# Fourteen products of ones on TensorE in the first stage of a fused attention and feed-forward kernel

## The chip, the core and the metric

The kernel runs on one core of a Trainium2 chip. The metric is the device time of one execution in microseconds; below, "us" means that. A run's time is the median of several executions; the profile shows one more execution, with its own time.

## What is computed

The inputs are q, k and v of 4 batches, 8 heads, 1152 positions and 64 dimensions, and two weight matrices. Neighbouring rows of q are averaged, so 576 rows of scores stand for each head:

```python
q_pool = q.reshape(B, H, S // 2, 2, D).mean(axis=3)
scores = np.matmul(q_pool, k.transpose(0, 1, 3, 2)) / np.sqrt(D)
attn = softmax(scores)                       # rows, max subtracted
x = np.matmul(attn, v).transpose(0, 2, 1, 3).reshape(B * S // 2, H * D)
h = x @ w_in                                 # 2304x512 by 512x2048
out = np.maximum(h, 0.0) ** 2 @ w_out        # 2304x512
```

## The kernel before

The work falls into 16 pairs of heads (4 batches by 4 pairs), each cut into nine chunks of 128 rows of scores, 144 chunks in all. A chunk goes through a fixed series of steps: a score product S on TensorE, a row bound MX on VectorE, the exponential EX on ScalarE, a transpose of the result P, and, for a group of chunks, the product with v. Behind the attention, and mixed into it, nine blocks of 256 rows go through the feed-forward part (lines 1032 and 1081 hold its products).

Pair 0 is treated in full 32-bit precision from the start. The load LK of k comes in three pieces (line 384), that of q (LQ) in one (line 376). KX (line 422) transposes k on TensorE in three groups of six products with the identity, and KC (lines 414 and 416) copies each to SBUF. QS (line 399) adds neighbouring rows of q on VectorE, QY (line 435) transposes the sums in two groups, and QC copies them. Then the first score group S (line 652) makes two chunks at once, and VectorE's bound MX (line 684) and ScalarE's exponential EX (line 708) follow. For the pairs 0 to 3, P is transposed on TensorE in three groups of three, TP (line 749), and copied by TC (line 759 on ScalarE, 761 on VectorE).

The pairs 1 to 4 also have bound products GR (line 465): nine products of the raw k (or q, or v) with itself, whose largest entry, read by GM (line 469) on VectorE, gives a scale. GR of k for pair 1 is the first of them; it waits for that pair's load of k (line 369). That load uses the buffer of pair 0's k, and so waits for the last KX.

Beside this the weights are loaded (line 1135) and turned from 64-bit to 32-bit numbers, in steps W0, W1, W2, W4, W5 for w_in and U0 to U5 for w_out, on ScalarE (lines 1143, 1149, 1162), VectorE (line 1152, the combine at line 1168, line 1177) and GpSimd.

All these steps are listed with what they depend on, and the string `ORDER` gives the one sequence in which they are put out, with the engine of each and the buffer or PSUM bank that it takes. So every engine has a fixed order of its own and waits only for data and buffers. TensorE's first steps are KX 0, KX 1, KX 2, QY 0, QY 1, S of the chunks 0 and 1, GR of k for pair 1, TP 0 and TP 1 of chunk 0, S of the chunks 2 and 3, TP 0 of chunk 1. On SyncE's queue the loads of pair 0's k and q and of the first piece of w_in stand first; then come k of pair 1, a piece of w_in, one of w_out, and q of pair 1. Two PSUM banks, called a, serve KX, QY, GR, TP and most else; a step takes one through `bank(o)`, and the step that has read it gives it back. `ones` is a column of 128 ones of 16-bit type, written by VectorE at line 1325, and `cfg(k, d)` reads an entry of the table CFG.

Of the kernel before, what the change touches and what calls it, by code (L numbers as in the profile page):

```python
# [16 lines left out]
AX = mybir.AxisListType  # L17
PSUM = bass.MemoryType.PSUM

CFG = {'SPLIT': 0, 'TURN': [], 'TURNB': [], 'WDP': ((1, 0), (1, 1), (1, 2), (1, 3)), 'WSP': 0.4394, 'WOF': 23.2581, 'MSP': 10.7319, 'FV': (0, 1, 2, 3), 'PART': 1, 'QXD': (1, 2, 3, 4), 'MSC': (0, 1, 2, 3, 4, 5, 6, 7, 8, 9, 10, 11, 12, 13, 14, 15), 'FS': (0,), 'NSG': (12, 13, 14, 15)}  # L20


def cfg(k, d):
    return CFG.get(k, d)

# [117 lines left out]
def kernel(  # L143
# [12 lines left out]
    nc = tc.nc  # L156
# [27 lines left out]
    ones = c_p.tile([128, 1], BF16, name="ones")  # L184
# [56 lines left out]
    def bank(o, *shape):  # L241
        r, x = plan.slot[o["name"]]
        t = banks[r][x]
        if not shape:
            return t
        return t[:, : shape[0] * shape[1]].rearrange("p (a b) -> p a b", a=shape[0])

    def buf(*key):
        r, x = plan.slot[key]
        return bufs[r][x]  # L250

    def raw(*key):
        return raws[plan.slot[key][1]]
# [41 lines left out]
    def qT(n):  # L295
        s = preps[n]["slot"]
        return qTs[s] if s is not None else buf("qT", n).rearrange("p (l c m) -> p l c m", l=2, c=9)

    def k4(n):
        return kT(n).rearrange("p a b -> p (a b)").bitcast(F32).rearrange("p (c k) -> p c k", c=9)  # L300

    def q4(t):
        return t.rearrange("p l c m -> p (l c m)").bitcast(F32).rearrange("p (c m) -> p c m", m=64)
# [43 lines left out]
    def prep(n):  # L347
# [11 lines left out]
        def rk():  # L359
            return raw("k", n).rearrange("p (h c d) -> p h c d", h=2, c=9)  # L360
# [47 lines left out]
        if n in full_s:  # L408
            assert not keep
            kt4, qt4 = k4(n), q4(qT(n))  # L410

            def move(o, out, x):
                if o["eng"] == "ACT":
                    nc.scalar.activation(out, x, AF.Copy)
                else:
                    nc.vector.tensor_copy(out, x)

            def kx(o, x):
                tl["kx", n, x] = t = bank(o, 3, 128)
                for y in range(3):  # L420
                    for h in range(2):
                        nc.tensor.matmul(
                            t[h * 64 : h * 64 + 64, y], lhsT=rk()[:, h, 3 * x + y, :], rhs=ident,
                            start=True, stop=True, skip_group_check=True,
                        )

            def kc(o, x):
                move(o, kt4[:, 3 * x : 3 * x + 3], tl.pop(("kx", n, x)))

            def qy(o, z):  # L430
                tl["qy", n, z] = t = bank(o, 5, 64)
                for y in range(5 - z):
                    for h in range(2):
                        hs = slice(h * 64, h * 64 + 64)
                        nc.tensor.matmul(t[hs, y], lhsT=rq()[:, 5 * z + y, 0, :], rhs=ident[:, h : h + 127 : 2], start=True, stop=True, skip_group_check=True)

            def qc(o, z):
                t = tl.pop(("qy", n, z))
                if z == 0:
                    move(o, qt4[:, :5], t)  # L440
                else:
                    move(o, qt4[:, 5:8], t[:, :3])
                    for h in range(2):
                        hs = slice(h * 64, h * 64 + 64)
                        move(o, qt4[hs, 9 + h], t[hs, 3])

            add(("QS", n), qse, [("LQ", n)], qsum, need)
            for x in range(3):
                add(("KX", n, x), {"PE": 1270}, [("LK", n) + ((x,) if n == 0 and x < 2 else ())] + old, lambda o, x=x: kx(o, x), need, take=(("KX", n, x), ("a",), 0), give=("k", n) if x == 2 else None)
                add(("KC", n, x), alt("KC", ACT=380, DVE=460), [("KX", n, x)] + old, lambda o, x=x: kc(o, x), need, give=("KX", n, x))  # L450
            for z in range(2):
                add(("QY", n, z), {"PE": 760 - 150 * z}, [("QS", n)] + old, lambda o, z=z: qy(o, z), need, take=(("QY", n, z), ("a",), 0), give=("q", n) if z else None)
                add(("QC", n, z), alt("QC", ACT=350 + 350 * z, DVE=400 + 300 * z), [("QY", n, z)] + old, lambda o, z=z: qc(o, z), need, give=("QY", n, z))
        gram_ = cfg("GR0", 1) <= n < cfg("GRN", 5)

        if gram_:

            def gram(o, i, nm):
                if ("acc", n) not in tl:
                    tl["acc", n] = sm_p.tile([128, 3], F32, tag="acc", name="acc", bufs=2)  # L460
                p = bank(o, 1, 128)
                t = raw(nm, n).bitcast(BF16).rearrange("p (f t) -> p f t", t=2)[:, :, 1]
                for c in range(9):
                    x = t[:, c * 128 : (c + 1) * 128]
                    nc.tensor.matmul(p[:, 0], lhsT=x, rhs=x, start=(c == 0), stop=(c == 8))
                tl["gm", n, nm] = p

            def gmax(o, i, nm):
                nc.vector.reduce_max(tl["acc", n][:, i : i + 1], tl.pop(("gm", n, nm)), axis=AX.X)

            for i, nm in enumerate("kqv"):
                if nm not in todo:
                    continue
                L = "L" + nm.upper()
                add(("GR", n, nm), {"PE": 560}, [(L, n)], lambda o, i=i, nm=nm: gram(o, i, nm), need, take=(("GR", n, nm), ("a",), 0))
                add(("GM", n, nm), {"DVE": 200}, [("GR", n, nm)], lambda o, i=i, nm=nm: gmax(o, i, nm), need, give=("GR", n, nm))
            if "q" in todo:
                add(("QS", n), qse, [("GR", n, "q")], qsum, need)
            fdep = [("GM", n, nm) for nm in "kqv"]
        else:  # L480

            def sq(o, i, nm):
                if ("acc", n) not in tl:
                    tl["acc", n] = sm_p.tile([128, 3], F32, tag="acc", name="acc", bufs=2)
                src = rq()[:, :, 0, :] if nm == "q" else rk() if nm == "k" else rv()
                if nm == "v":
                    j = v2s[slot][:, :, :, 0, :].bitcast(BF16)
                else:
                    j = buf(nm + "2", n)[:, :1152].bitcast(BF16).rearrange("p (h c d) -> p h c d", h=2, c=9)
                    j = j[:, 0] if nm == "q" else j  # L490
                nc.scalar.activation(j, src, AF.Square, accum_out=tl["acc", n][:, i : i + 1])

            if "k" in todo:
                add(("QS", n), qse, [("LQ", n)], qsum, need)
                add(("QK", n), {"ACT": 1200}, [("LK", n)], lambda o: sq(o, 0, "k"), need, take=ktake)
            if "v" in todo:
                add(("QV", n), {"ACT": 1200}, [("LV", n)] + oldv, lambda o: sq(o, 2, "v"), need)
            if "q" in todo:
                add(("QQ", n), {"ACT": 700}, [("QS", n)], lambda o: sq(o, 1, "q"), need, take=qtake)
            fdep = [("QK", n), ("QQ", n), ("QV", n)]  # L500
# [123 lines left out]
    def chunk(i):  # L624
# [117 lines left out]
        if n in full_v:  # L742
            pt = pslot(vi, j, True)

            def tp4(o, x):
                t = bank(o, 3, 128)
                for y in range(3):
                    c = 3 * x + y
                    nc.tensor.matmul(  # L749
                        t[:, y], lhsT=P()[:, c * 128 : (c + 1) * 128], rhs=ident, is_transpose=True,  # L750
                        start=(y == 0), stop=(y == 2), skip_group_check=True,
                    )
                tl["tp", i, x] = t

            def tc4(o, x):
                t = tl.pop(("tp", i, x))
                out = pt[:, 3 * x : 3 * x + 3]
                if o["eng"] == "ACT":
                    nc.scalar.activation(out, t, AF.Copy)  # L759
                else:  # L760
                    nc.vector.tensor_copy(out, t)

            for x in range(3):
                add(("TP", i, x), {"PE": 400}, [("EX", i)] + ring + ([("TP", i, x - 1)] if x else []), lambda o, x=x: tp4(o, x), i, take=(("TP", i, x), ("a",), 0), give=("P", i) if x == 2 else None)
                add(("TC", i, x), alt("TC", ACT=380, DVE=460), [("TP", i, x)] + ring, lambda o, x=x: tc4(o, x), i, give=("TP", i, x))
            return
# [603 lines left out]
```

## Time and profile before

| | us |
|---|---|
| median of 3 runs | 772.78 |
| lowest and highest run | 770.53, 773.82 |
| the profiled execution | 774.11 |
| its span, from the first to the last instruction | 772.30 |
| the rest of that execution, outside the span | 1.81 |

The profile shows for each engine what it did when, and what ended each of its idle times. TensorE has two rows: PE for products and PEld for weight loads, which run beside them. A product of 32-bit numbers appears as two instructions, so KX's 18 products are 36. A duration in a row of the timeline runs from the first start to the last end of the instructions that the row merges; neighbouring rows overlap a little, since products are pipelined. "Idle before" names the time for which the engine had nothing to do, and the instruction that ended it. The granted clock is that of TensorE, as a share of 2.4 GHz.

### The profile page before, as it was taken

What the parts mean: (1) busy time and instruction counts of PE and PEld (TensorE: products, weight loads), DVE (VectorE), ACT (ScalarE), POOL (GpSimd) and SP (SyncE); (2) the same over time, 40 slices, a digit from 0 to 9 for tenths busy, and PEclk for the clock granted to TensorE, in tenths of its full rate; (3) what the DMA queues carried; (4) which work ended last, traced back from release to release, by engine and by line L of the source; (5) the groups of instructions that cost most, each with busy time, mean ns of one, the idle gap of its engine ahead of it and who ended that gap; (6) DMA issues with size and microseconds to landing.
All of it is one profiled execution on the core that took longest, in us unless ns stands there. A gap on an engine that the chain in (4) does not pass through costs nothing.

```text
span 772.3 us, 15204 instructions
## 1 busy us (share of the span) xinstructions
PE 735.6 (95%) x5998; PEld 484.1 (63%) x5998; DVE 580.4 (75%) x983; ACT 525.7 (68%) x830; POOL 314.9 (41%) x221
## 2 busy tenths in 40 slices
PE   6799899999999999999999999999999999999997
PEld 4555556557756775577656856675577558576763
DVE  5998998899988887788989989887768872424032
ACT  6899978889876796698867886874798542323020
POOL 0434322456455454673452354544665431122001
PEclk9999999999999999999999999999999999999999
DMA  8895672629999999999999999998999936001011
GB/s 303 279 269 170 166 214 86 123 76 220 202 205 206 218 210 230 191 201 208 229 201 224 199 222 208 191 209 181 188 205 174 189 76 121 1 1 28 2 28 28
DMA packets 324584, 128.96 MB, mean 167 GB/s; under 512 B 306848, under 2 KB 307616, under 8 KB 324512
## 3 DMA queue, kind: packets, MB, share of 16 engines
q1 hardware_dynamic: 324512, 127.98, 79.8%
q8 instruction: 47, 0.77, 0.4%
q14 instruction: 25, 0.20, 0.1%
HBM read 45.09 MB, written 4.72 MB: 64 GB/s over the span
## 4 chain that ended last, share of the span: by engine, by line
PE 64%; DMA 11%; DVE 9%; ACT 6%; issue 6%; POOL 3%; SPq 0%; DVEq 0%; ACTq 0%; POOLq 0%
PE ba L1081 16%; PE ba L1032 10%; PE s L673 9%; PE ba L868 8%; PE bt L1032 7%; PE bt L1081 5%; DMA PT<-buf 4%; DVE s L684 3%; PE ba L860 3%; DMA raw<-in_q_dram 2%; ACT buf L708 2%; PE ba L749 2%; DMA kT<-buf 2%; POOL buf L720 1%; ACT PT L759 1%
## 5 line engine op out<-in xcount | busy, mean ns | idle before, releaser
L684 DVE TENSOR_SCALAR_CACHE_REDUCE s<-s,esc 128x1152 f32<-128x1152 f32 x135 | 190.5, 1420 | 29.9 <-PE s L673 26.2
L708 ACT ACTIVATE buf<-s,ca 128x1152 f32<-128x1152 f32 x144 | 175.0, 1216 | 44.8 <-POOL ca L694 16.1
L1032 PEld LDWEIGHTS <-w 128*128 128x128 f16 x1728 | 167.2, 98 | 27.1 <-issue 4.3
L720 POOL TENSOR_TENSOR buf<-buf,buf 128x1152 f16<-128x1152 f32 x49 | 121.1, 2474 | 86.7 <-ACT buf L712 53.3
L1081 PE MATMUL ba<-w,region 128*128 128x512 f16 x672 | 154.6, 382 | 0.3 <-ACT ru L930 0.3
L1081 PEld LDWEIGHTS <-region 128*128 128x128 f16 x864 | 83.2, 99 | 96.6 <-issue 3.7
L673 PE MATMUL s<-kT,qT 128*128 128x512 f16 x720 | 135.3, 328 | 3.0 <-ACT buf L708 1.4
L1032 PE MATMUL ba<-region,w 128*128 128x256 f16 x1056 | 121.2, 273 | 2.0 <-DVE xs L989 1.2
L673 PEld LDWEIGHTS <-qT 128*128 128x128 f16 x720 | 63.6, 100 | 59.8 <-issue 10.1
L1059 POOL TENSOR_TENSOR region<-region 128x512 f16<-128x512 f32 x37 | 47.7, 1291 | 119.4 <-DVE region L1055 75.6
L720 DVE TENSOR_TENSOR buf<-buf,buf 128x1152 f16<-128x1152 f32 x59 | 83.0, 1412 | 6.2 <-ACT buf L712 2.6
L868 PE MATMUL ba<-PT,v 128*64 128x320 f16 (+1 forms) x1296 | 84.3, 287 | 0.3 <-DMA PT<-buf 0.3
L868 PEld LDWEIGHTS <-v 128*64 128x64 f16 x1296 | 70.8, 110 | 13.2 <-issue 6.3
L712 ACT ACTIVATE buf<-buf 128x1152 f16<-128x1152 f32 x62 | 71.6, 1156 | 7.4 <-DMA PT<-buf 3.5
L1047 ACT ACTIVATE region<-region 128x512 f16<-128x512 f32 x72 | 44.1, 624 | 34.5 <-DVE region L1044 34.1
L749 PE MATMUL ba<-ident,buf 128*128 128x128 f32 x324 | 52.8, 287 | 12.0 <-ACT PT L759 6.2
L1032 PE MATMUL bt<-region,w 128*128 128x256 f16 x480 | 53.9, 273 | 0.0
L749 PEld LDWEIGHTS ba<-ident,buf 128*128 128x128 f32 x324 | 34.1, 142 | 28.3 <-ACT PT L759 11.2
L282 POOL TENSOR_SCALAR buf<-buf,cols 128x1152 f16<-128x1152 f32 x24 | 34.2, 1428 | 29.6 <-ACT buf L708 26.1
L1081 PE MATMUL bt<-w,region 128*128 128x512 f16 x192 | 43.6, 379 | 0.0
L759 ACT ACTIVATE PT<-ba 128x384 f32<-128x384 f32 x81 | 37.2, 489 | 8.5 <-PE ba L749 8.1
L1042 ACT ACTIVATE region<-bt 128x512 f32<-128x512 f32 x11 | 6.4, 593 | 49.1 <-PE bt L1032 26.4
(191 smaller groups left out, 922.3 us busy)
## 6 DMA issues: line engine op xcount, KB each, us to landing
raw<-in_q_dram SPq DMA_DIRECT2D x16, 576.0 KB, 5.2
raw<-in_k_dram SPq DMA_DIRECT2D x15, 576.0 KB, 5.1
region<-in_moe_w_in_dram SPq DMA_DIRECT2D x8, 1024.0 KB, 6.8
w<-in_moe_w_out_dram SPq DMA_DIRECT2D x8, 1024.0 KB, 5.7
raw<-in_v_dram SPq DMA_DIRECT2D x12, 576.0 KB, 4.4
v<-in_v_dram SPq DMA_DIRECT2D x4, 576.0 KB, 8.5
out_dram<-half SPq DMA_DIRECT2D x18, 128.0 KB, 2.5
out_dram<-buf SPq DMA_DIRECT2D x18, 128.0 KB, 2.4
```

The source lines that it names most:

```text
L673: nc.tensor.matmul(s[:, x, :w], lhsT=qt[:, l].rearrange("p c m -> p (c m)")[:, 128 * c0 + h : 128 * c0 + h + 255 : 2], rhs=rhs, **st)
L684: nc.vector.tensor_scalar(st3(), st3(), sc, 3e38, op0=ALU.mult, op1=ALU.min, accum_out=a[:, x : x + 1])
L708: nc.scalar.activation(P(), st3(), AF.Exp, bias=a[:, 1:2], scale=s1, accum_out=col)
L712: nc.scalar.activation(hl()[:, 0], P(), AF.Copy)
L720: e.tensor_tensor(out=hl()[:, 1], in0=P(), in1=hl()[:, 0], op=ALU.subtract)
L749: nc.tensor.matmul(t[:, y], lhsT=P()[:, c * 128 : (c + 1) * 128], rhs=ident, is_transpose=True, start=(y == 0), stop=(y == 2), skip_group_ ...
L759: nc.scalar.activation(out, t, AF.Copy)
L868: nc.tensor.matmul(px[h * 64 : (h + 1) * 64, 64 * r * (1 - h) : 64 * r * (1 - h) + N], lhsT=vv[:, h, kc, vl, :], rhs=p2(vi, r, h, 9 * pl + ...
L1032: nc.tensor.matmul(ph[:, f2], lhsT=w16[0][:, SLOT[f // 4], wl, a, f % 4 * 128 : (f % 4 + 1) * 128], rhs=xhl()[:, xl, a], start=(i == 0), s ...
L1047: nc.scalar.activation(gt[u][:, 0], rt[u % 2], AF.Square)
L1059: e.tensor_tensor(out=gt[u][:, 1], in0=rt[u % 2], in1=gt[u][:, 0], op=ALU.subtract)
L1081: nc.tensor.matmul(p[:, :DM], lhsT=g[:, gl, f % 2, tt * 128 : (tt + 1) * 128], rhs=w16[1][:, SLOT[f // 4], wl, f % 4], start=(f == 0 and g ...
```

## The change

CFG gets an entry BUSY, which names three steps and a count for each: five for the first KX of pair 0, five for GR of k of pair 1, four for the first TP of chunk 0. A new function puts out that many products of the ones, 128 by 128 as weights and 128 by 512 as the moving operand, into the bank of the step, right after the bank is taken and ahead of the step's own products, which write over the result. QY calls it too, but has no count.

```diff
-CFG = {'SPLIT': 0, ...
+CFG = {'BUSY': {('KX', 0, 0): 5, ('GR', 1, 'k'): 5, ('TP', 0, 0): 4}, 'SPLIT': 0, ...
...
+    def busy(o):
+
+        for _ in range(cfg("BUSY", {}).get(o["name"], 0)):
+            nc.tensor.matmul(bank(o), lhsT=ones.to_broadcast([128, 128]), rhs=ones.to_broadcast([128, 512]), start=True, stop=True)
+
...
             def kx(o, x):
                 tl["kx", n, x] = t = bank(o, 3, 128)
+                busy(o)
...
             def qy(o, z):
                 tl["qy", n, z] = t = bank(o, 5, 64)
+                busy(o)
...
                 p = bank(o, 1, 128)
+                busy(o)
                 t = raw(nm, n).bitcast(BF16).rearrange("p (f t) -> p f t", t=2)[:, :, 1]
...
             def tp4(o, x):
                 t = bank(o, 3, 128)
+                busy(o)
```

## Rows read from the trace of the kernel before

**Rows 1.** The page: the chain that ended last, shares of the span by engine.

```profile
PE 64%; DMA 11%; DVE 9%; ACT 6%; issue 6%; POOL 3%; SPq 0%; DVEq 0%; ACTq 0%; POOLq 0%
```

**Rows 2.** The chain in order of time: start us, us, what.

```profile
2.26 4.88 DMA raw<-in_q_dram
...
7.16 0.77 DVE raw L399
...
11.74 2.16 DVE s L684 x3
```

**Rows 3.** Timeline of TensorE's products: start us, us, line, names, count.

```profile
3.44 4.11 PE L422 MATMUL ba<-ident,raw 128*64 128x128 f32 x36 [3.44 <-DMA raw<-in_k_dram]
...
8.02 1.27 PE L435 MATMUL ba<-ident,raw 128*64 128x64 f32 x36 [0.47 <-DVE raw L399]
...
9.48 2.21 PE L652 MATMUL s<-kT,qT 64*128 64x512 f32 x12 [0.19 <-DVE qT L416]
...
13.13 0.69 PE L465 MATMUL ba<-raw 128*128 128x128 bf16 x9 [1.45 <-DMA raw<-in_k_dram]
...
14.54 1.33 PE L749 MATMUL ba<-ident,buf 128*128 128x128 f32 x6 [0.72 <-ACT buf L708]
...
15.80 3.42 PE L652 MATMUL s<-kT,qT 64*128 64x512 f32 x12
...
19.15 0.88 PE L749 MATMUL ba<-ident,buf 128*128 128x128 f32 x6
```

**Rows 4.** One line's weight loads: ns min/median/max, first and last start.

```profile
L422 PEld LDWEIGHTS ba<-ident,raw x36: 181/231/231, 3.4 to 6.9; 128*64 128x64 f32 x36
...
L435 PEld LDWEIGHTS ba<-ident,raw x36: 132/136/140, 8.0 to 9.0; 128*64 128x64 f32 x36
```

**Rows 5.** Windows of 0.5 us: TensorE busy, granted clock, DMA share, GB/s.

```profile
4.50:5.00 0.50, 0.50 (x10) 1.00 0.73 212
...
14.50:15.00 0.50, 0.46 (x3) 0.81 1.03 401
...
15.00:15.50 0.50, 0.50 (x5) 0.50 1.01 410
...
18.00:18.50 0.50, 0.50 (x4) 0.77 0.93 265
```

**Rows 6.** Waits of SyncE's queue, first 30 us: total, times, longest.

```profile
SPq L369 <- PE ba L422: 1.8, 1, 1.8
```

**Rows 7.** Timeline of ScalarE.

```profile
10.00 1.15 ACT L1143 ACTIVATE w<-region 128x1024 f32<-128x1024 f32 x1
...
19.37 1.13 ACT L1143 ACTIVATE w<-w 128x1024 f32<-128x1024 f32 x1
...
22.35 0.50 ACT L759 ACTIVATE PT<-ba 128x384 f32<-128x384 f32 x1
```

**Rows 8.** Timeline of VectorE.

```profile
0.81 0.06 DVE L1325 MEMSET ones<- 128x1 bf16 x1 [0.81 <-PEq L1354]
...
15.91 0.56 DVE L761 COPY PT<-ba 128x384 f32<-128x384 f32 x1 [0.17 <-PE ba L749]
...
19.25 1.36 DVE L684 TENSOR_SCALAR_CACHE_REDUCE s<-s 128x1152 f32<-128x1152 f32 x1
...
20.54 2.10 DVE L1168 SCALAR_TENSOR_TENSOR w<-w 128x1024 int32<-128x1024 int32 x1
```

**Rows 9.** Timeline of TensorE, around 520 us.

```profile
516.97 2.75 PE L1081 MATMUL ba<-w,region 128*128 128x512 f16 x12
...
522.48 0.35 PE L504 MATMUL ba<-acc,cols 128*128 128x2 f32 x2 [1.79 <-DVE region L1044]
...
522.70 4.44 PE L1081 MATMUL ba<-w,region 128*128 128x512 f16 x12
```

**Rows 10.** Windows of 20 us: busy PE, PEld, DVE, ACT, POOL; clock, DMA share, GB/s.

```profile
320.00:340.00 20.00, 18.59 (x170) 12.44 (x167) 16.71 (x37) 15.38 (x24) 15.14 (x12) 0.91 1.09 211
...
520.00:540.00 20.00, 18.21 (x137) 10.48 (x137) 15.60 (x24) 8.80 (x16) 9.44 (x7) 0.91 0.83 180
```

More of the change, by code (lines that the diff above doesn't have):

```diff
@@ L18 @@
 PSUM = bass.MemoryType.PSUM
-CFG = {'SPLIT': 0, 'TURN': [], 'TURNB': [], 'WDP': ((1, 0), (1, 1), (1, 2), (1, 3)), 'WSP': 0.4394, 'WOF': 23.2581, 'MSP': 10.7319, 'FV': (0, 1, 2, 3), 'PART': 1, 'QXD': (1, 2, 3, 4), 'MSC': (0, 1, 2, 3, 4, 5, 6, 7, 8, 9, 10, 11, 12, 13, 14, 15), 'FS': (0,), 'NSG': (12, 13, 14, 15)}
+CFG = {'BUSY': {('KX', 0, 0): 5, ('GR', 1, 'k'): 5, ('TP', 0, 0): 4}, 'SPLIT': 0, 'TURN': [], 'TURNB': [], 'WDP': ((1, 0), (1, 1), (1, 2), (1, 3)), 'WSP': 0.4394, 'WOF': 23.2581, 'MSP': 10.7319, 'FV': (0, 1, 2, 3), 'PART': 1, 'QXD': (1, 2, 3, 4), 'MSC': (0, 1, 2, 3, 4, 5, 6, 7, 8, 9, 10, 11, 12, 13, 14, 15), 'FS': (0,), 'NSG': (12, 13, 14, 15)}
 def cfg(k, d):
```

## The prediction

> **What bounds the kernel now.** I read the chain of waits first. Over the whole span two thirds of it is TensorE's own work [rows 1], but the change acts in the first 16 us of 772, so the question is what the chain runs through there. In order of time it goes through the load of q of pair 0 (2.26 to 7.14 us), VectorE's pair sum at 7.16, and on to the first bound at 11.74 [rows 2]; the load of k and its transposes, which the first five products stand ahead of, are not in it. Next TensorE's timeline [rows 3]: the transposes of k (L422) run from 3.44 to 7.55, then the engine is idle 0.47 until the pair sum is done. It is idle again for 1.45 before pair 1's bound products (L465) at 13.13 and for 0.72 before the transposes of P (L749) at 14.54. These are the places where the change puts its products.
>
> Then the clock. The granted clock goes from full (2.4 GHz) to half (1.2 GHz) within 14.5 to 15.0, is 0.50 after that, and is back within 18.0 to 18.5 [rows 5]. What that costs stands in TensorE's timeline: six transposes take 1.33 at 14.54 and 0.88 at 19.15; the twelve instructions of a score group take 3.42 at 15.80 and 2.21 at 9.48 [rows 3]. So 0.45 + 1.21 = 1.66 us of TensorE time are lost there.
>
> The recorded clock is 1.00 at 4.5 to 5.0 as well [rows 5], yet the weight loads of L422 have a median of 231 ns there, and those of L435, of the same shape and type, 136 ns from 8.0 on [rows 4]. By these durations the transposes of k run at the low level, and I take 1.00 there for a record that begins before the first change of level. The Trainium skill (TensorE: Matmul & The Clock Gate, Part 1) says that the throttled clock is the default and that activity releases it, and warns that the recorded clock events can be unreliable. By the recorded clock the first five products can give L422 nothing; by the durations and that rule, up to half of its time; the sum below is the same for both.
>
> Last, what follows. ScalarE works back to back from 10.00 to 22.85, sixteen rows from the first to the last with no idle time noted between them [rows 7], and VectorE from its bound at 11.74 [rows 2] to its combine at 20.54 has one gap, 0.17 at 15.91 [rows 8]. So in the stretch where the clock is low, TensorE is not the bound: VectorE and ScalarE, each in its fixed order, are.
>
> **The change part by part.** It removes and moves nothing. It adds 5 + 5 + 4 products of 512 columns with their weight loads to TensorE. No DMA, no wait of another engine and no new bank is added: each product writes the bank that its step holds anyway, and is overwritten. Price of one product: 2.75 / 12 = 0.23 us from a row of 512-column products at the full clock; at the low level twice that, 0.46, is a safe upper bound, since a row that lies mostly at the low level gives 4.44 / 12 = 0.37 [rows 9].
>
> *Five ahead of the first transposes of k.* They need only the ones, written at 0.81 [rows 8], and a bank that nobody has used. At the low level they take at most 5 x 0.46 = 2.3 and end by about 3.2, before the k load ends TensorE's wait at 3.44 [rows 3]. Cost: nothing, hidden by the load. If TensorE started later than I think, L422 would be late, but it has 0.47 of idle time behind it before L435, so up to that nothing follows. Gain: the clock may rise earlier. Then L422's 4.11 shrinks to between 2.05 (full clock throughout) and 4.11 (no change), and it ends between 5.5 and 7.55. I take about 6, since the rise will come during L422, not before it. Who sees that? L435 at 8.02 waits for the pair sum, and that for the load of q: it does not move. What does move is the SyncE queue: the load of k of pair 1 waited 1.8 us for L422 [rows 6], and behind it stand one load of w_in, one of w_out and the load of q of pair 1 (that one waits for L435 too). They can start up to about 1.8 earlier. Their users are in ScalarE's and VectorE's fixed orders, which are full. Value on the path: zero.
>
> *Five ahead of pair 1's bound products.* The bank was freed by a copy that the first score group, at 9.48, waits for as well, so they follow the first score group at 11.7 and take 5 x 0.23 = 1.15, to 12.85. The k load of pair 1 lets L465 start at 13.13. Cost: nothing while the clock is full; if that load lands 1 us earlier, L465 still starts no later than now.
>
> *Four ahead of the transposes of P.* TensorE is free from 13.13 + 0.69 = 13.82; 4 x 0.23 = 0.92 gives 14.74 against 14.54, so the transposes start 0.20 late. At the full clock the six of them then take 0.88 in place of 1.33 and end at 15.62, against 15.87 now. VectorE's copy at 15.91, which waited 0.17, can start at 15.74, when the instruction before it ends: a gain of 0.17. The score group behind it ends at about 15.6 + 2.2 = 17.8, 1.4 earlier than now. But its reader, VectorE's bound at 19.25, came there in VectorE's order without a wait, and the next instruction, the combine at 20.54, waits for ScalarE's instruction of 19.37, which ends at 20.50 [rows 7, 8]. ScalarE's run began at 10.00, before anything that the change moves. So the 0.17 is gone at 20.54, and the 1.4 before it.
>
> Sum: 0 on the path, at the most 0.17. The profiled execution, 774.11 (span 772.30 and 1.81 around it), would become 774.0; it lies 1.3 above the median of the runs, 772.78, so I forecast **772.6** for the median.
>
> **The rivals.** *One: the early gain turns into a fall of the clock ahead of the first scores.* With L422 ending at 5.5 to 6.5, TensorE waits 1.5 to 2.5 for the pair sum, where it waited 0.47. Idle times of this size precede the falls now: 1.45 + 0.72 before the one at 14.5; 1.79 before the row of 4.44 at 522.70 [rows 9], in a window of lower mean clock [rows 10]. If it falls near 8, L435 (1.27) at most doubles, +1.27, and the first score group takes 3.42, +1.21. These are on the chain: VectorE's first bound waits for that group [rows 2], and ScalarE's first exponential for the bound. +2.5 gives 775.1, slower. It decides if the idle time ahead of L435 passes about 1.5 with the clock already high. For it: the sizes above. Against: if the clock rises late in L422, the idle stays short, and L422 stands directly before it.
>
> *Two: the time won at 14.5 to 18.5 does reach the end.* 1.66 less 0.20 for the late start is 1.46: 771.2. For it: TensorE has two thirds of the chain. Against: the order of VectorE and ScalarE above.
>
> *Three: the products do not hold the clock, and it is at the low level when the four before L749 run.* Then they take up to 4 x 0.46 = 1.84, L749 starts at 15.66, 1.1 late, and the bound at 19.25 gets its scores at 15.66 + 1.33 + 3.42 = 20.4: +1.15, 773.8. For it: no row shows such products holding the clock. The Trainium skill (same title, Part 4) says that transposes on TensorE do not count as activity as other products do; by it the six transposes may let the clock fall anyway. No row here separates the two.
>
> *Four: the two later falls move.* Windows of 20 us with a mean clock of 0.91 stand at 320 and at 520 [rows 10]. The one at 522.70 costs 4.44 - 2.75 = 1.69 [rows 9]. The change adds nothing there, but a shift of a microsecond may move them. Both gone: at most 2 x 1.69 = 3.4, 769.3; a third one new: 774.3.
>
> **How the numbers follow.** The forecast has 0.52, rival one 0.2, two 0.12, three 0.06, four 0.1. A measurement of this kernel can tell about 0.5%, 3.9 us, from no change. No single case passes it: they lie between 769.3 and 775.1. It takes two together, such as two with both later falls gone (767.8), or one with a new later fall (776.8). I give 0.1 to faster by over 0.5%, 0.82 to within, 0.08 to slower. The runs before spread from 770.53 to 773.82 without any change, so the range reaches from 769.8, which holds rival two and most of four, to 775.4, which holds one.
>
> **What would show it.** Right: products from about 0.9 to 3.2, L422 shorter than 4.11, L435 still near 8.0 and the first scores near 9.5; the granted clock full from 8 to 20; the second score group in about 2.2; VectorE's bound still at about 19.2 and its combine at 20.5. Wrong if L435 or the first score group shows weight loads near 231 ns (rival one), if the clock still falls at 14.5 to 15.0 (three), or if VectorE's instructions after 20.5 and ScalarE's after 22.9 stand over 1 us earlier than now (two).

## The result, and the profile after

The median is 778.30 us over six runs (776.03 to 780.61); the kernel before, run beside it, has 773.84. The ratio is 1.0068, with a 95% interval of 1.0040 to 1.0096: slower, by 4.5 us, where 772.6 and no change were forecast. The profiled execution of after took 776.03, with a span of 774.2 against 772.30 before. Here and below, medians and ratios leave out the few executions that took over 1.5% longer than the fastest of the same kernel: one each of again, n28 and n64, two of n96.

First the page of after: the span, the busy times, the queue that brings instructions, and the chain's shares.

```profile
span 774.2 us, 15231 instructions
...
PE 737.1 (95%) x6011; PEld 483.7 (62%) x6012; DVE 579.2 (75%) x983; ACT 525.0 (68%) x830; POOL 316.6 (41%) x221
...
q8 instruction: 47, 0.77, 0.4%
...
PE 37%; DMA 2%; issue 1%; POOL 1%; ACT 1%; DVE 1%; SPq 0%; POOLq 0%; DVEq 0%; ACTq 0%
```

The printed shares of the chain add up to 43% of the span, those of [rows 1] to 99%: this chain was followed over less than half of it, and the two aren't to be compared. The third line matters below: 47 transfers with 0.77 MB, 16 KB each, and the page of before has the same line. (A second queue of this kind, q14, has 25 transfers with 0.20 MB before and 26 after.)

Next the timeline of TensorE's products (start us, us, engine, line), which answers to [rows 3]. After's line numbers are up to 9 higher: L428 is KX, L442 QY, L660 S, L473 GR, L758 TP, and L251 the added products.

```profile
0.93 2.32 PE L251 MATMUL ba<-ones 128*128 128x512 bf16 x5 [0.93 <-DVE ones L1334]
3.56 1.87 PE L428 MATMUL ba<-ident,raw 128*64 128x128 f32 x24 [0.31 <-DMA raw<-in_k_dram]
6.41 0.88 PE L428 MATMUL ba<-ident,raw 128*64 128x128 f32 x12 [0.98 <-DMA raw<-in_k_dram]
8.58 1.27 PE L442 MATMUL ba<-ident,raw 128*64 128x64 f32 x36 [1.29 <-DVE raw L404]
10.04 2.21 PE L660 MATMUL s<-kT,qT 64*128 64x512 f32 x12 [0.19 <-DVE qT L421]
12.41 1.04 PE L251 MATMUL ba<-ones 128*128 128x512 bf16 x4 [0.16 <-issue]
13.58 0.69 PE L473 MATMUL ba<-raw 128*128 128x128 bf16 x9
14.11 1.03 PE L251 MATMUL ba<-ones 128*128 128x512 bf16 x4
15.11 0.87 PE L758 MATMUL ba<-ident,buf 128*128 128x128 f32 x6
15.91 2.71 PE L660 MATMUL s<-kT,qT 64*128 64x512 f32 x12
...
21.33 1.12 PE L473 MATMUL ba<-raw 128*128 128x128 bf16 x9 [1.89 <-ACT PT L768]
```

The five early products run from 0.93 to 3.25, and KX no longer needs 4.11 us of work but 1.87 + 0.88, with 0.98 between for the last piece of k. The transposes of P take 0.87 instead of 1.33, the second score group 2.71 instead of 3.42. (A record of one product ahead of GR is missing.) The timeline of VectorE shows what that is worth, at the bound and the combine of [rows 8].

```profile
19.64 1.36 DVE L692 TENSOR_SCALAR_CACHE_REDUCE s<-s 128x1152 f32<-128x1152 f32 x1
...
20.93 2.09 DVE L1177 SCALAR_TENSOR_TENSOR w<-w 128x1024 int32<-128x1024 int32 x1
```

The combine starts 0.39 later than before, and so in these two executions the early stage gained nothing and lost little. The windows of 0.5 us (TensorE busy, granted clock, DMA share, GB/s), beside [rows 5], show where the fall of the clock went.

```profile
14.50:15.00 0.50, 0.50 (x3) 1.00 0.94 360
...
21.50:22.00 0.50, 0.50 (x7) 0.50 0.75 238
...
24.50:25.00 0.50, 0.50 (x3) 0.73 0.99 383
```

It isn't gone; in this execution it stands at 21.4 to 24.8 instead of 14.8 to 18.2. Neither that nor the shorter times are shown to be the products' work. The run less14 below has none of the products, and its profile has the same times at other places, with the fall at 22.5:

```profile
16.42 0.87 PE L758 MATMUL ba<-ident,buf 128*128 128x128 f32 x6 [1.47 <-ACT buf L716]
17.23 2.71 PE L660 MATMUL s<-kT,qT 64*128 64x512 f32 x12
```

None of this is 4.5 us, so the loss lies later, and the experiments look for what carries it there.

### The profile page after: what moved, and what is told of

It reads as the page before. It is cut to its first block, busy times and chain, and to the rows that moved or that the text cites. A ratio compares the mean times of both kernels' runs of the same rounds, so it can differ in the third digit from the quotient of the medians.

```text
span 774.2 us, 15231 instructions
## 1 busy us (share of the span) xinstructions
PE 737.1 (95%) x6011; PEld 483.7 (62%) x6012; DVE 579.2 (75%) x983; ACT 525.0 (68%) x830; POOL 316.6 (41%) x221
## 5 line engine op out<-in xcount | busy, mean ns | idle before, releaser
L1090 PE MATMUL ba<-w,region 128*128 128x512 f16 x672 | 152.9, 379 | 0.3 <-ACT ru L939 0.3
L758 PE MATMUL ba<-ident,buf 128*128 128x128 f32 x324 | 53.3, 289 | 8.4 <-ACT PT L768 5.3
L758 PEld LDWEIGHTS ba<-ident,buf 128*128 128x128 f32 x324 | 34.5, 143 | 25.1 <-ACT PT L768 10.4
L287 POOL TENSOR_SCALAR buf<-buf,cols 128x1152 f16<-128x1152 f32 x24 | 34.1, 1422 | 30.9 <-ACT buf L716 22.5
```

The lines of the kernel that those rows point to most:

```text
L758: nc.tensor.matmul(t[:, y], lhsT=P()[:, c * 128 : (c + 1) * 128], rhs=ident, is_transpose=True, start=(y == 0), stop=(y == 2), skip_group_ ...
L1090: nc.tensor.matmul(p[:, :DM], lhsT=g[:, gl, f % 2, tt * 128 : (tt + 1) * 128], rhs=w16[1][:, SLOT[f // 4], wl, f % 4], start=(f == 0 and g ...
```

## The experiments

Four batches, each beside runs of the kernel before (medians 773.18, 772.72, 772.53, 772.46, from 25 to 35 runs each). In the first eight only the entry BUSY differs from after.

**One part alone, and one single product.**

```diff
 kx5   CFG = {'BUSY': {('KX', 0, 0): 5}, ...
 gr5   CFG = {'BUSY': {('GR', 1, 'k'): 5}, ...
 tp4   CFG = {'BUSY': {('TP', 0, 0): 4}, ...
 kx1   CFG = {'BUSY': {('KX', 0, 0): 1}, ...
```

> Only the five products ahead of the first transposes of k. If the cost sits in one group of products and it is this one (through the loads that are queued behind the last transposes of k), the time is 4 to 5 us above the kernel before (ratio about 1.006). If the cost sits in another group, the ratio is 0.998 to 1.002. If the time only reflects how later transfers happen to fall after any small early shift, the ratio can be anything from 0.998 to 1.007, and the ratios of the three parts do not add up to that of the whole.

> Only the five products ahead of pair 1's bound products. If the cost sits here, ratio about 1.006. If it sits in another group: TensorE was idle for 1.45 us there and the products take 1.1, so nothing before the transposes of P moves, and the fall of the clock at 14.5 us may go: ratio 0.998 to 1.001. If any small early shift does it: 0.998 to 1.007.

> Only the four products ahead of the first transposes of P. If the cost sits here (the transposes start 0.2 us late, VectorE's copy behind them too), ratio about 1.006. If it sits elsewhere, 0.999 to 1.002. If any small early shift does it: 0.998 to 1.007.

> One product of ones ahead of the first transposes of k, over by about 1.5 us, two microseconds before k is there. It moves no step of the work. If the cost of the change is one of steps that are moved, or of the clock, the ratio is 0.999 to 1.001. If a few more instructions in TensorE's stream are by themselves what costs time, it is about 1.006, as with the whole change.

Measured: kx5 775.24, ratio 1.0019 [0.9994, 1.0044]; gr5 774.59, 1.0025 [0.9999, 1.0052]; tp4 774.81, 1.0021 [0.9999, 1.0043]; kx1 772.35, 0.9996 [0.9973, 1.0020]. No part costs 4.5 us. Three unlike parts (before the k load lands, behind the first scores, ahead of P) cost about the same, 1.4 to 2.1 us, though each interval still reaches 1. That speaks against any one place in the first 16 us.

**Two parts, and the whole once more.**

```diff
 again CFG = {'BUSY': {('KX', 0, 0): 5, ('GR', 1, 'k'): 5, ('TP', 0, 0): 4}, ...
 kx_gr CFG = {'BUSY': {('KX', 0, 0): 5, ('GR', 1, 'k'): 5}, ...
 kx_tp CFG = {'BUSY': {('KX', 0, 0): 5, ('TP', 0, 0): 4}, ...
 gr_tp CFG = {'BUSY': {('GR', 1, 'k'): 5, ('TP', 0, 0): 4}, ...
```

> The whole change once more, on the chip and beside the same runs as the pairs of parts. If the parts each cost 0.2 per cent and add up, the ratio is 1.006 to 1.008. If the first measurement of six runs stood high by chance, and the change only moves where the clock falls, it is 0.999 to 1.004.

> Without the four products ahead of the transposes of P. Parts that add up: 1.004. A cost that needs all three (or that is the third's): 0.999 to 1.002. Chance alone: 0.998 to 1.003.

> Without the five products ahead of pair 1's bound products. Parts that add up: 1.004. A cost that needs all three: 0.999 to 1.002. Chance alone: 0.998 to 1.003.

> Without the five products ahead of the transposes of k. Parts that add up: 1.0045. A cost that needs all three: 0.999 to 1.002. Chance alone: 0.998 to 1.003.

Measured: again 776.42, 1.0052 [1.0029, 1.0076]; kx_gr 776.60, 1.0047 [1.0024, 1.0069]; kx_tp 777.23, 1.0053 [1.0030, 1.0075]; gr_tp 778.12, 1.0065 [1.0041, 1.0089]. The loss is there again, and any two parts make about all of it. Costs that add up aren't excluded by this: the single parts sum to 3.5, 3.7 and 3.0 for the pairs, where 3.9, 4.5 and 5.4 were measured, and to 5.1 for the whole. What the pairs have in common is the number of instructions that they add to TensorE's stream (a product and its weight load each): 20, 18 and 18, against 8 to 10 for one part and 28 for the whole. This gave the theory of the next batch: what costs isn't what the products do; it is that every later instruction of TensorE moves back in the stream, and with it the moments at which the 16 KB transfers of instructions fall.

**Fourteen products that do nearly nothing, twice as many, and the change with its stream brought back to the old length.** In n14 and n28 all stand ahead of KX, where TensorE waits for k anyway (14 of them ran from 0.92 to 1.85). In comp and less14, fourteen products of w_in's bound (at 28 and 35 us) are left out, so that part of that bound isn't computed.

```diff
 n14   CFG = {'BUSY': {('KX', 0, 0): 14}, ...         n28: 28
-            nc.tensor.matmul(bank(o), lhsT=ones.to_broadcast([128, 128]), rhs=ones.to_broadcast([128, 512]), start=True, stop=True)
+            nc.tensor.matmul(bank(o)[:32, :64], lhsT=ones.to_broadcast([128, 32]), rhs=ones.to_broadcast([128, 64]), start=True, stop=True)
 comp  BUSY as in after; less14  CFG = {'BUSY': {}, ...; in both, in the loop of w_in's bound products:
+                            if w == 0 and (i == 0 and a in (1, 2, 3) or i == 1 and c < 2 and a == 1):
+                                continue
...
-                                p[:, c * 128 : (c + 1) * 128], lhsT=x, rhs=x, start=(a == 0), stop=(a == 3)
+                                p[:, c * 128 : (c + 1) * 128], lhsT=x, rhs=x, start=(a == 0), stop=(a == (0 if w == 0 and i == 0 else 3))
```

> The kernel before plus 14 narrow products of ones (32 columns of weights, 64 of moving data) ahead of the first transposes of k, done before k is there. As many instructions more in TensorE's stream as the whole change has (28), but no product in the idle times at 11.7 and 13.8 us. If the cost comes from where the loads of TensorE's instructions fall among the other transfers (the stream behind them is shifted by 28), the ratio is 1.004 to 1.006. If it comes from what the wide products do to the clock or to the first 16 us, 0.999 to 1.001.

> 28 narrow products there, 56 instructions more. Position of the instruction loads: another place, so the ratio may be anything from 0.998 to 1.008, but it need not be that of the kernel before. Clock or the first 16 us: 0.999 to 1.001.

> The whole change, less 14 of the 32 products of the bounds of the first two quarters of w_in at 28 and 35 us, so that TensorE's stream behind them stands as in the kernel before. It leaves out part of that bound; TensorE is not the limit there. Position of the instruction loads: back to 0.998 to 1.002. Clock or the first 16 us: 1.004 to 1.006 as with the whole change.

> The kernel before less the same 14 products of the bounds, with none of the change, so that the stream behind 35 us is shifted by 28 instructions the other way. It leaves out the same part of the bound. Position of the instruction loads: can lie off 1.000 to either side, 0.994 to 1.006. Clock or the first 16 us: 0.999 to 1.001. It is also the reference for the kernel with the whole change less these products.

Measured: n14 778.19, 1.0086 [1.0052, 1.0119]; n28 777.93, 1.0073 [1.0046, 1.0099]; comp 772.87, 1.0004 [0.9985, 1.0024]; less14 774.57, 1.0032 [1.0004, 1.0059]. This is the decisive batch. Products without work cost as much as the whole change, if there are as many of them; and the whole change, with all its work and its clock, costs 0.3 us (interval -1.2 to +1.9) once 28 instructions are taken out soon after it. So the first 16 us come to nothing that can be measured, as forecast, and the count of instructions has the price. That 28 fewer cost 2.0 (interval 0.3 to 4.6, less14) says that it is a matter of position, not of more. One doubt about n14 can be set aside: in its profile QY and the first scores run at the low level, the trace's record of the clock has full speed from 12.2 on, and the combine starts at 22.21, 1.7 later than before. But in again and n142, which lose 3.7 and 6.9, it starts at 20.77 and 20.65.

**A whole transfer's worth of instructions.** TensorE's products and weight loads, 5998 + 5998 on the page of before, over 47 transfers are 255 for one. Counted in the trace of before, TensorE starts 253 instructions in the mean between one load and the next (156 to 340). After, the loads come at the same counts (2 later in the mean), and so some 28 instructions earlier in the work. If position is all, 256 more instructions must bring every load back to where it was, and 284 must act like 28.

```diff
 n128  CFG = {'BUSY': {('KX', 0, 0): 60, ('QY', 0, 0): 8, ('GR', 1, 'k'): 36, ('TP', 0, 0): 16, ('GR', 1, 'q'): 8}, ...
 n142  CFG = {'BUSY': {('KX', 0, 0): 62, ('QY', 0, 0): 8, ('GR', 1, 'k'): 40, ('TP', 0, 0): 20, ('GR', 1, 'q'): 12}, ...
 n64   CFG = {'BUSY': {('KX', 0, 0): 40, ('GR', 1, 'k'): 24}, ...
 n96   CFG = {'BUSY': {('KX', 0, 0): 50, ('QY', 0, 0): 4, ('GR', 1, 'k'): 30, ('TP', 0, 0): 12}, ...
 all four with the narrow product of n14
```

> 128 narrow products in the idle times of the first 21 us, 256 instructions more in TensorE's stream, as many as one 16 KB load of instructions seems to bring (those loads stand 256 instructions apart in the mean). If the cost is set by where these loads fall, they now fall where they fell before: ratio 0.999 to 1.003, the upper part for what the products themselves may delay. If each instruction added costs time, or any change of the first stage does, 1.005 or more.

> 142 narrow products, 284 instructions: one load more and 28 over, as the whole change has. Position of the loads: 1.004 to 1.010, like the whole change and the 14 narrow products. No period: like the one with 128, within 0.002.

> 64 narrow products, 128 instructions, half a load. Position of the loads: another place, 0.996 to 1.008; under 0.998 would be a place better than that of the kernel before. A cost for each instruction: above the 1.007 of 28 products.

> 96 narrow products, 192 instructions, three quarters of a load. Position of the loads: another place, 0.996 to 1.008. A cost for each instruction: above the 1.007 of 28 products.

Measured: n128 772.65, 1.0010 [0.9985, 1.0034]; n142 779.33, 1.0086 [1.0054, 1.0119]; n64 774.26, 1.0034 [1.0005, 1.0062]; n96 775.81, 1.0035 [1.0007, 1.0064]. The cost has the period of a transfer: 128 products more cost nothing that can be measured, and 14 more on top of them cost 6.7 us. The page of n128 shows the one transfer more that this takes, 48, in its busy row and its row of that queue:

```profile
PE 738.2 (95%) x6126; PEld 488.9 (63%) x6126; DVE 584.6 (75%) x983; ACT 525.8 (68%) x830; POOL 316.5 (41%) x221
...
q8 instruction: 48, 0.79, 0.4%
```

**Where the time goes.** VectorE has the same 983 instructions in the same order in every kernel. So a stretch can be timed from the start of one of them to the start of another, and compared with the same two before. Most of the difference between after and before falls in four stretches, and in steps. The columns give us against the profiled execution of before, for the stretches that lie there at 185.58 to 206.72 (S), 270.24 to 301.53 (C), 445.65 to 467.77 (B) and 600.23 to 618.72 (A); the last column is what the runs measured, median against the median beside it. The four are picked for their differences, not taken at random.

| kernel | instructions added | S | C | B | A | sum | runs |
|---|---|---|---|---|---|---|---|
| comp | 0, net | -0.4 | 0.1 | -0.2 | 0.0 | -0.5 | +0.3 |
| kx1 | 2 | -0.1 | 0.0 | -0.1 | 0.0 | -0.2 | -0.8 |
| n128 | 256 | 0.3 | 0.0 | -0.1 | -0.2 | 0.0 | +0.2 |
| tp4 | 8 | -0.1 | 1.8 | -0.1 | 0.0 | 1.6 | +1.6 |
| gr5 | 10 | -0.2 | 1.2 | 0.0 | 0.8 | 1.8 | +1.4 |
| kx5 | 10 | -0.1 | 1.8 | -0.2 | 0.7 | 2.2 | +2.1 |
| kx_tp | 18 | 2.4 | 1.1 | 0.0 | 0.8 | 4.3 | +4.5 |
| gr_tp | 18 | 2.4 | 2.1 | 0.0 | 0.8 | 5.3 | +5.4 |
| kx_gr | 20 | 2.6 | 1.2 | 0.0 | 1.0 | 4.8 | +3.9 |
| again | 28 | -0.5 | 1.0 | 0.0 | 0.8 | 1.3 | +3.7 |
| after | 28 | -0.5 | 2.1 | 3.3 | 0.9 | 5.8 | +4.5 |
| n14 | 28 | 2.4 | 1.8 | 3.2 | 1.0 | 8.4 | +5.7 |
| n142 | 284 | -0.5 | 1.8 | 3.3 | 0.8 | 5.4 | +6.9 |
| n28 | 56 | -0.5 | 0.0 | 2.3 | 0.3 | 2.1 | +5.4 |

One execution each stands against medians of several, and a kernel differs from execution to execution: again lost 2.4 and kx5 1.6 at 402 to 446, which no other did, and n28's runs lost more than these stretches show, n14's less. For the others in the table sum and runs agree within 1.5, and the three kernels whose loads of instructions are back where before has them, or nearly, are within 0.4 of zero in every column. (n64 has 1.8, 0.8, 1.5, 0.6, 4.7 in sum where the runs lost 1.8; n96 -0.1, 0.9, 0.2, 0.9, and the runs 3.3; less14 -0.5, 0.7, 1.0, 0.2, and the runs 2.0.) The sums aren't the differences of the spans: comp's profiled span is 5.4 shorter than before's, n128's 2.5 longer. Outside the four stretches the profiles differ too, by falls of the clock among other things, and the runs of the kernel before alone spread from 767.17 to 777.20.

*What a load does to a transposition.* The profile gives the time from the issue of a DMA to its landing. Every kernel issues the same 138 transpositions by DMA, so each one's time can be compared over the 18 traces. Call usual its median in the kernels where no load of instructions starts near it (from 1.5 us before the issue to 2 us after the landing; 1169 cases). Where a load starts between the issue and the usual landing (236 cases), the transposition lands later than usual by 0.8 us in the median, and in 80% of the cases by over 0.3. With none near, 3% are that late. This is what the stretches A to C show one by one.

*Stretch A* is the plainest. The timeline of TensorE's products with v, before, and the row of the instruction queue in the window 607.8 to 608.0:

```profile
605.85 0.32 PE L868 MATMUL ba<-PT,v 128*64 128x320 f16 x1
606.51 3.72 PE L868 MATMUL ba<-PT,v 128*64 128x320 f16 x52 [0.34 <-DMA PT<-buf]
```

```profile
q8 instruction: 1, 0.02, 50.4%
```

The same after, with the window 606.0 to 606.2:

```profile
606.83 0.32 PE L877 MATMUL ba<-PT,v 128*64 128x320 f16 x1
...
608.40 2.77 PE L877 MATMUL ba<-PT,v 128*64 128x320 f16 x38 [1.25 <-DMA PT<-buf]
```

```profile
q8 instruction: 1, 0.02, 35.7%
```

TensorE waits for a transposed P that a DMA brings. Before, the load of instructions comes 1.3 us after the wait is over; after, it comes before it is over, and the wait is 1.25 instead of 0.34. Counted from the VectorE instruction that opens the stretch, the load stands at 7.6 in before, comp, kx1, tp4 and n128, and A costs -0.2 to 0.0; it stands at 4.9 to 5.1 in the nine kernels with 10, 18, 20, 28 and 284 instructions more, and A costs 0.7 to 1.0 in each of them. The transposition in question takes 5.8 from issue to landing before and 6.7 after, 5.7 to 5.8 in the five and 6.5 to 6.8 in the nine. Further off it is mixed: n28 (0.2) and less14 (7.9) pay 0.3 and 0.2, n96 (9.6) and n64 (11.9) 0.9 and 0.6, so this load isn't the only thing that can cost there: in n64 and n96 that transposition takes 5.8 too, but is issued late.

*Stretch B* is the dearest. Before, the timeline of all engines, SyncE's transposition of q among them, and the instruction queue at 450.2 to 450.4:

```profile
444.65 1.31 SPq L559 DMA_TRANSPOSE qT<-buf  x1
...
448.49 2.46 DVE L568 COPY qT<-qT 64x1152 f16<-64x1152 f16 x1
...
449.09 1.15 PE L673 MATMUL s<-kT,qT 128*128 128x512 f16 x6
...
455.40 1.17 ACT L491 ACTIVATE v<-raw 128x1152 bf16<-128x1152 f32 x1 [0.36 <-DMA raw<-in_v_dram]
...
466.24 1.15 PE L673 MATMUL s<-kT,qT 128*128 128x512 f16 x6
```

```profile
q8 instruction: 1, 0.02, 31.5%
```

and the transposition at 444.65 in the list of DMA issues, with its us from issue to landing:

```profile
qT<-buf SPq DMA_TRANSPOSE x1, 3.4
```

After, with the window 449.8 to 450.0:

```profile
446.82 1.32 SPq L567 DMA_TRANSPOSE qT<-buf  x1
...
450.28 1.15 PE L681 MATMUL s<-kT,qT 128*128 128x512 f16 x6
...
452.00 0.46 DVE L576 COPY qT<-qT 64x1152 f16<-64x1152 f16 x1 [2.34 <-DMA qT<-buf]
...
459.67 1.16 ACT L499 ACTIVATE v<-raw 128x1152 bf16<-128x1152 f32 x1 [3.11 <-DMA raw<-in_v_dram]
...
462.33 1.14 PE L681 MATMUL s<-kT,qT 128*128 128x512 f16 x6 [0.81 <-ACT buf L716]
...
470.74 1.15 PE L681 MATMUL s<-kT,qT 128*128 128x512 f16 x6 [1.44 <-DMA kT<-buf]
```

```profile
q8 instruction: 1, 0.02, 30.1%
```

```profile
qT<-buf SPq DMA_TRANSPOSE x1, 5.2
```

Before, the copy starts 3.84 after the transposition of q is issued, without a wait, and the load of instructions comes later still, 5.6 after the issue. After, the load comes 3.2 after it, before the transposition has landed, and the copy starts 5.18 after it, with a wait of 2.34. The late copy alone isn't what costs: counted from VectorE's bound that opens the stretch, it starts 5.2 after it here, and 5.0 in kx_gr, kx_tp, gr_tp and again, where B costs nothing. What they don't have is the delay behind it on SyncE's queue: the next transposition of P takes 3.54 there instead of 2.46 (2.56 to 2.61 in those four), the load of v stands behind it, is issued 6.2 after the bound instead of 4.4, and lands 12.8 after it instead of 9.7. ScalarE waits 3.11 for it instead of 0.36, TensorE then 0.81 for the exponential and 1.44 for the transposition of k. From the first score product shown to the last are 17.15 us before (449.09 to 466.24) and 20.46 after (450.28 to 470.74): 3.31 lost on TensorE itself. n14 and n142 have the load at the same place, 3.1 behind the issue, the transposition of q lands after 5.1 and 5.0, and the waits are the same (2.31 and 2.13, 3.08 and 3.30, 0.81 each, 1.42 and 1.44). With the load 1.8 and 1.6 behind the issue, n28 and n64 land it after 4.5 and pay 2.3 and 1.5. From 3.5 on (kx_tp; kx_gr 3.6, kx5 4.4, again 4.6, eight more up to 6.2) it lands after 3.3 to 3.4, and B costs nothing, but for less14, which pays 1.0 with the load at 6.2.

*Stretch S* turns an early landing into a loss. The timelines of VectorE, GpSimd and TensorE, before:

```profile
197.94 0.68 DVE L1059 TENSOR_TENSOR region<-region 128x512 f16<-128x512 f32 x1
198.81 2.37 POOL L720 TENSOR_TENSOR buf<-buf,buf 128x1152 f16<-128x1152 f32 x1 [4.67 <-ACT buf L712]
...
200.50 0.35 PE L504 MATMUL ba<-acc,cols 128*128 128x2 f32 x2 [0.29 <-DVE region L261]
```

and in n14:

```profile
197.23 2.40 POOL L728 TENSOR_TENSOR buf<-buf,buf 128x1152 f16<-128x1152 f32 x1 [3.62 <-ACT buf L720]
197.38 2.80 DVE L1068 TENSOR_TENSOR region<-region 128x512 f16<-128x512 f32 x1
...
202.07 0.35 PE L512 MATMUL ba<-acc,cols 128*128 128x2 f32 x2 [2.17 <-DVE region L266]
```

Before, a transposition of P at 189.49 takes 6.00 on SyncE's queue, with the load of instructions 4.1 behind its start; in n14 that at 189.24 has the load 0.8 behind its start and takes 4.59. From issue to landing they take 8.0 and 6.7. So GpSimd's split, which follows on it through ScalarE, starts ahead of VectorE's and VectorE's takes 2.80 instead of 0.68; TensorE's product at 202.07 then waits 2.17 for VectorE, where it waited 0.29. It is so in n14, kx_gr, kx_tp and gr_tp, the four with 2.4 to 2.6 in column S. In after and again GpSimd starts 0.10 and 0.16 behind VectorE, and S costs nothing.

*Stretch C* starts with a transposition of P, issued at 263.54 before and at 262.57 after. Before, TensorE's score product at 272.11 waits for nothing; after, ScalarE waits 1.45 for a transposed P, TensorE 0.97 for ScalarE, and GpSimd's split at 272.70 meets one of VectorE and takes 2.30:

```profile
268.89 1.16 ACT L720 ACTIVATE buf<-buf 128x1152 f16<-128x1152 f32 x1 [1.45 <-DMA PT<-buf]
...
272.15 1.14 PE L681 MATMUL s<-kT,qT 128*128 128x512 f16 x6 [0.97 <-ACT buf L716]
272.63 1.35 DVE L728 TENSOR_TENSOR buf<-buf,buf 128x1152 f16<-128x1152 f32 x1
272.70 2.30 POOL L1068 TENSOR_TENSOR region<-region 128x512 f16<-128x512 f32 x1 [1.39 <-ACT region L1061]
...
278.08 0.69 DVE L1053 TENSOR_SCALAR region<-ba 128x512 f32<-128x512 f32 x1 [2.51 <-POOL region L1068]
```

The list of DMA issues has this transposition with its us from issue to landing, before and after:

```profile
PT<-buf SPq DMA_TRANSPOSE x1, 4.6
```

```profile
PT<-buf SPq DMA_TRANSPOSE x1, 6.3
```

C follows the count (1.8 with 8, 1.0 to 2.1 with 28, 0 with 0, 2 or 256). The load next to it falls at about the same place in all of these, 4.0 to 4.5 behind the issue and so close to the landing. Still the kernels part in two: in before, comp, kx1 and n128 the transposition lands after 4.6 and the load takes 1.1 to 1.4; in the ten with 8, 10, 18, 20, 28 and 284 instructions it lands after 6.2 to 6.4, the load takes 0.9 to 1.0, and ScalarE waits 1.4 to 1.6. That reads as if the one that comes first made the other wait. No row shows the order, and why a small difference in place decides it stays open.

Last, why the spans of the two profiles differ by 1.9 alone. Before's execution holds the fall of the clock at 522.70 [rows 9]; after's doesn't, and its rows there are

```profile
525.03 0.34 PE L512 MATMUL ba<-acc,cols 128*128 128x2 f32 x2
525.22 2.75 PE L1090 MATMUL ba<-w,region 128*128 128x512 f16 x12
```

From 501.98 to 545.40 before took 3.7 longer than the same VectorE instructions of after. The 5.8 lost and the 3.7 won leave 2.1, and the spans differ by 1.9. Whether that fall is there varies between executions (it is missing in comp and in again too); the medians carry it on both sides.

## Why the prediction was wrong

**The step that failed** is the sentence "No DMA, no wait of another engine and no new bank is added". Word for word it is true, 47 loads of instructions before and after; what failed is what I took from it, that no transfer behind the first 16 us is touched. The fourteen products and their weight loads are instructions, and instructions come by DMA: 28 more in the stream move each later load of 16 KB ahead in the work by 28 instructions. I took the stream as free, put everything behind the early stage at nothing but for the clock, and costed the products alone. The runs have 4.5 us there, and the profile of after has them in transpositions that land late where a load falls into them (A, B and C). By n14 the instructions without the products' work cost 5.7 us, and by comp the products' work with the stream's length restored costs 0.3, which can't be told from nothing.

**Rival four** came near it ("The change adds nothing there, but a shift of a microsecond may move them"), but for the clock alone, and with 3.4 us as the most. The falls did move: the 20 us windows at 320 and 520 have a clock of 1.00 after. That was a gain in the profiled execution alone (again, the same kernel, has falls at 321.8 and 417.4 in its profile), and the kernel was slower all the same.

**The sum of the early stage held**: a gain of 0 to 0.17 forecast, +0.3 (interval -1.2 to +1.9) by comp, of which the fourteen products left out there, at 1.08 for sixteen, can hide 0.9 at most; VectorE was 0.39 late at 20.93, which says little, since that combine starts at 20.40 to 22.99 in the 18 profiles, and at 22.99 in less14, without any of the products. (By the printed forecast rivals two and four come to 771.1 and 769.2, each 0.1 lower than written.) Point by point:

- Five ahead of KX: 0.93 to 3.25, as forecast (0.9 to 3.2), and L422's work shrank as the low clock of its weight loads [rows 4] suggested: their median is 137 ns after, 231 before, and the windows have 1.00 in both. With the same five products it is 137 in again too, but 194 in kx_tp and 226 to 230 in kx5, comp and kx_gr, so the gain isn't certain. The trace's record of the clock has its first entry, full speed, at 4.29 after and at 7.99 before; the 1.00 ahead of it stands for no entry, as the prediction took it. The Trainium skill (TensorE: Matmul & The Clock Gate, Part 1) warns that recorded clock events can be unreliable; here the entries that the record has agree with the durations. L422's products ended at 7.29 instead of about 6, since the last piece of k landed late.
- QY at 8.58 instead of 8.0: its wait is for VectorE's pair sum, which started at 7.72 when the load of q landed. That load landed between 7.03 and 8.02 in the profiles taken, with or without the change.
- Five ahead of GR and four ahead of TP: TP at 15.11 instead of 14.74, since the load of q had put the first scores 0.56 back, in 0.87 (0.88 forecast). The score group took 2.71 instead of 2.2, at a recorded clock of 1.00, and what was gained there ended at VectorE's combine, as forecast.
- Rival one: no fall near 8, though TensorE was idle 0.98 and 1.29 ahead of QY. Rival three: no fall at 14.5 to 15.0 after, but the products needn't be the reason; less14 without them has its fall at 22.5, and kx5 with five of them at 16.4. That this point came out right may be luck. Rival two fails too: VectorE isn't earlier after 20.5.

**The range** was wrong with the step: 769.8 to 775.4 was the spread of the runs and of a few clock events. No row that I had read was about instruction loads, though the page of before names their queue.

## What to carry to other kernels

A few instructions more or fewer on the busiest engine shift where its instruction loads fall in all later work, and here that was worth 0 to 7 us, against nothing that could be measured for what the instructions did. So an edit worth under 1% is measured beside a control that adds as many instructions with nearly no work, and one that brings the stream back to its old length. Where a kernel leans on DMA transposes, the position is a knob of its own: a few idle products early, up to one transfer's worth, can be tried for the best one. None of the counts tried here was faster than the kernel before by more than the noise.

## What was not expected of the hardware

- TensorE's instructions come in transfers of 16 KB, 47 over this span, one for some 255 products and weight loads; 256 more make it 48. Where one falls against a transposition by DMA decides when that lands: in B 5.0 to 5.2 us from issue to landing instead of 3.3 to 3.4, in C 6.2 to 6.4 instead of 4.6, in A 6.5 to 6.8 instead of 5.7 to 5.8. On SyncE's queue the transposition in S takes 5.6 to 6.0 with the load 3.7 to 4.1 behind the start and 4.1 to 4.6 with it 0.5 to 0.8 behind.
- VectorE and GpSimd slow each other: VectorE's split takes 2.80 instead of 0.68 when GpSimd's starts just ahead, its copy of q 2.46 instead of 0.46, and GpSimd's split 2.30 instead of 1.16. The Trainium skill (GPSIMD Engine Reference, Specifications) says that GpSimd shares its SBUF interfaces with VectorE and contends with VectorE's instructions that have two SBUF inputs or run in a 2-port mode. The trace agrees for the split, which has two inputs; the copy has one, and no row shows whether it ran in such a mode.
- Where the first fall of the clock stands differs from profile to profile: 14.8 before, 21.4 after, 16.4 in kx5 with five of the products, 24.0 in kx1 with one, 22.5 in less14 with none. So no run here shows that the idle products moved it.
